# Causal convolution and ELU block: band read without a reversing copy, w_in in three pieces, live rows only, halo zeroed earlier

## The chip, the cores and the metric

The kernel runs on one core of one Trainium2 chip. The metric is the device time of the slowest core, which here is the only one, in microseconds (us). Runs of one kernel agree within about 0.3%. A profiled execution has its own span, which is 2.1 to 2.4 us shorter than the time of the same run, so spans are compared with spans and times with times.

The engines by their names in the profile: PE multiplies matrices, and PEld is its loading of weights; ACT, DVE and POOL compute element by element; SP only issues transfers. A transfer (DMA) is carried by up to 16 DMA engines and counts up a semaphore, on which an instruction that needs the data waits. "Head" below is the time before group 1 starts, and "halo" the 6 rows of zeros ahead of a sequence.

## The reference

x is [8, 4096, 192] in float32. Each of 8 heads of 24 channels is filtered along the sequence with 7 taps (a softmax of its row of `weight`), causally, with zeros ahead of each of the 8 sequences. The result, 32768 rows of 192, goes through two matmuls with an ELU between them:

```python
x_pad = np.concatenate([np.zeros((B, pad, D)), x], axis=1)      # pad = 6
idx = np.arange(S)[:, None] + np.arange(K)[None, :]
x_unf = x_pad[:, idx, :].reshape(B, S, K, H, group)
out = np.einsum('hk,bskhg->bshg', softmax(weight), x_unf)       # then [32768, 192]
h = out @ w_in                                                  # 192 -> 2048
g = np.where(h > 0.0, h, np.exp(np.minimum(h, 0.0)) - 1.0)
return g @ w_out                                                # 2048 -> 192
```

## The kernel before

The 32768 rows are worked through in 32 groups of 1024 rows. A group has 16 steps; step n = 16 s + i makes 128 of the 2048 hidden columns for group s. In each step PE makes h (`H<-att,w_in`), ACT the exponential, POOL the clamp, DVE joins them into gT, and some steps later PE multiplies gT by w_out. The convolution is a matmul too: rows of x (`xg`, windows of 118 rows that overlap by 6, 112 new ones each) against a band matrix `Tm` that holds each head's taps shifted by one from partition to partition. It is made one to two groups ahead; group 0 is done differently, and the first convolution by `Tm` stands in step 7.

The band is built in DRAM. The tap row goes there between zeros, and one transfer reads it with a step of one element per partition. That gives it reversed, so DVE turns it round:

```python
sy.dma_start(bass.AP(tensor=taps.tensor, offset=CW, ap=[[CW, HEADS], [1, CW]]), zt[:, :]).then_inc(s_band, 16)
W(s_band, 32)
sy.dma_start(Tr[:, :, :].rearrange("p h e -> p (h e)"),
    bass.AP(tensor=taps.tensor, offset=TAP + 1, ap=[[1, P], [1, HEADS * CW]])).then_inc(s_band, 16)
...
W(s_band, 48)                                       # DVE, before its first gT
v.tensor_copy(Tm[:], Tr[:, :, ::-1]).then_inc(s_tm)
```

POOL's queue loads and casts the weights and the first two groups of x, in this order, before POOL's first clamp:

```python
W(s_wd, 16)
load_w_in(0, (0, 1))            # columns 0:512, both partition halves
load_w_in(1, (0, 1))            # columns 512:2048
load_x(1, 0); load_x(1, 1)      # 128 rows x 5 windows each
g.dma_start(w_out ...)
load_x(2, 0); load_x(2, 1)
for n in range(NP):
    if i == X_PAD and s + 2 < NS and (s + 2) % SPB == 0:   # X_PAD = 8
        pad_x(s + 2)            # zero the 6 halo rows of a sequence's first group
    ...                         # two clamps
```

From the fourth group on, POOL casts x into DRAM (`x_cast`), and SP loads it from there, 128 rows of four windows and 70 of the fifth:

```python
for w0, w1, rows in ((0, WPG - 1, P), (WPG - 1, WPG, GS - TOK * (WPG - 1) + PAD)):
    sy.dma_start(xg[0:rows, s % NXB, v0 + w0 : v0 + w1, :],
        bass.AP(tensor=xb.tensor, offset=(row + TOK * w0) * D,
                ap=[[D, rows], [TOK * D, w1 - w0], [1, D]])).then_inc(s_xq[s % NXB][part], 16)
```

Of the kernel before, what the change touches and what calls it, by code (L numbers as in the profile page):

```python
# [12 lines left out]
P = 128  # L13
HP = 64
# [11 lines left out]
GS = 512  # L26
SUP = 2 * GS
PAD = KSIZE - 1
NXB = 2
NE = 4  # L30
NG3 = 2
# [3 lines left out]
    ((0, (0, 15, 8, 9)), (1, (6, 6, 7, 13))),  # L35
)
RUN = 4
WCOLS = ((0, 512), (512, 2048))
Q_PART = (0,) * 4 + (1,) * 12
WARM = (9, 1)  # L40

CONV_AT = ((0, 1, 1, 0), (4, 1, 1, 1), (9, 2, 0, 0), (12, 2, 0, 1))
# [4 lines left out]
QUAD = 4  # L47
XTW = 136
HALO = 2
X_PAD, X_COPY, X_LOAD = 8, 3, 15  # L50
X_LATE = (13, 18)


def bass_lightweight_conv__then__act_elu_kernel(
# [160 lines left out]
            t, half = divmod(n_half - 1, 2)  # L215
            previous[n_half // 2, n_half % 2, 0, g] = (t, half, 0, g)

    taps = nc.dram_tensor("conv_taps", ((HEADS + 2) * CW,), BF16).ap()

    xb = nc.dram_tensor("x_cast", (NT, D), BF16).ap()  # L220

    with ExitStack() as stack:
        def sbuf(name, shape, dt):
            return stack.enter_context(nc.sbuf_tensor(name, shape, dt))
# [4 lines left out]
        def sema(name):  # L229
            return stack.enter_context(nc.semaphore(name))  # L230
# [11 lines left out]
        whr = sbuf("whr", [HEADS, 1], FP32)  # L242
        sel = sbuf("sel", [HEADS, P], BF16)
        xg = sbuf("xg", [P, NXB, 2 * WPG, D], BF16)
        Tr = sbuf("Tr", [P, HEADS, CW], BF16)
        Tm = sbuf("Tm", [P, HEADS, CW], BF16)
        csb = sbuf("csb", [P, 2, 3 * 2 * WPG * HP], BF16)
        att = sbuf("att", [P, 2, 3, WPG * TOK], BF16)
# [9 lines left out]
        H = psum("H", [P, 3, 2 * GS])  # L258
        ops = psum("ops", [P, 2, GS])

        s_w = [sema(f"s_w{i}") for i in range(3)]
        s_wd = sema("s_wd")
        s_xl = [sema(f"s_xl{i}") for i in range(2)]
        s_xh = sema("s_xh")
        s_xha = sema("s_xha")
        s_wp = sema("s_wp")
        s_wb = sema("s_wb")
        s_tm = sema("s_tm")
        s_xb = [sema(f"s_xb{i}") for i in range(2)]
        s_xq = [[sema(f"s_xq{i}_{g}") for g in range(2)] for i in range(NXB)]  # L270
        s_id = sema("s_id")
# [42 lines left out]

        def x_ready(W, s, part):
            if s <= NXB:
                W(s_x[s % NXB][part], 16)
            else:
                W(s_xq[s % NXB][part], 32 * ((s - 1) // NXB))

# [73 lines left out]
        @block.gpsimd  # L394
        def _gpsimd(g: bass.BassGpSimd):
            W = Waits(g)

            def load_x(s, part):
                g.dma_start(  # L399
                    xg[:, s % NXB, WPG * part : WPG * (part + 1), :],  # L400
                    bass.AP(
                        tensor=x_flat.tensor,
                        offset=(s * SUP + GS * part - PAD) * D,
                        ap=[[D, P], [TOK * D, WPG], [1, D]],
                    ),
                ).then_inc(s_x[s % NXB][part], 16)

            def pad_x(s):
                x_ready(W, s, 0)
                g.memset(xg[0:PAD, s % NXB, 0, :], 0.0).then_inc(s_z)  # L410

            def copy_x(s):
                W(s_cv, 4 * (s - NXB - 1) + 1)
                if s == NXB + 1:
                    g.dma_start(  # L415
                        xb[s * SUP - 8 : s * SUP, :], x_flat[s * SUP - 8 : s * SUP, :]
                    ).then_inc(s_xb[s % 2], 16)
                g.dma_start(  # L418
                    xb[s * SUP : (s + 1) * SUP, :].rearrange("(p t) d -> p (t d)", p=P),
                    x_flat[s * SUP : (s + 1) * SUP, :].rearrange("(p t) d -> p (t d)", p=P),  # L420
                ).then_inc(s_xb[s % 2], 16)

            def load_w_in(k, halves):
                c0, c1 = WCOLS[k]
                for r in halves:
                    g.dma_start(  # L426
                        w_in[HP * r : HP * (r + 1), :, c0:c1],
                        moe_w_in.rearrange("(p j) f -> p j f", j=3)[:, :, c0:c1],
                    ).then_inc(s_w[k], 16)

            W(s_one, 1)
            g.affine_select(
                out=ident[:],
                in_=ident[:],
                pattern=[[-1, P]],
                compare_op=ALU.is_equal,
                fill=0.0,
                base=0,
                channel_multiplier=1,
            ).then_inc(s_id)  # L440
            g.affine_select(
                out=sel[:].rearrange("p (r h c) -> p r h c", r=2, h=HEADS),
                in_=sel[:].rearrange("p (r h c) -> p r h c", r=2, h=HEADS),
                pattern=[[0, 2], [-1, HEADS], [0, 8]],
                compare_op=ALU.is_equal,
                fill=0.0,
                base=0,
                channel_multiplier=1,
            ).then_inc(s_id)
            W(s_wd, 16)  # L450
            load_w_in(0, (0, 1))
            load_w_in(1, (0, 1))
            load_x(1, 0)
            load_x(1, 1)
            g.dma_start(
                w_out.rearrange("p (q r) d -> p q (r d)", r=RUN),
                moe_w_out.rearrange("(q p r) d -> p q (r d)", p=FC, r=RUN),
            ).then_inc(s_w[2], 16)
            load_x(2, 0)
            load_x(2, 1)  # L460
            for n in range(NP):
                s, i = divmod(n, NQ)
                if i == X_PAD and s + 2 < NS and (s + 2) % SPB == 0:
                    pad_x(s + 2)
                if i == X_COPY and s and s + 3 < NS:
                    copy_x(s + 3)
                if n == X_LATE[0]:
                    copy_x(3)
                for u in range(2):
                    W(s_exp, 2 * n + u + 1)  # L470
                    g.tensor_scalar(  # L471
                        out=E[:, n % NE, u, :],
                        in0=E[:, n % NE, u, :],
                        scalar1=1.0,
                        scalar2=0.0,
                        op0=ALU.min,
                        op1=ALU.max,
                    ).then_inc(s_clp)
# [72 lines left out]
        def _vector(v):  # L551
# [17 lines left out]
            W(s_v, 4)  # L569
            v.tensor_scalar(  # L570
                out=zt[:, TAP : TAP + KSIZE],
                in0=whe[:],
                scalar1=whr[:, 0:1],
                scalar2=None,
                op0=ALU.mult,
            ).then_inc(s_wp)
            W(s_xl[1], 16)
            v.tensor_copy(xh[:, 1, :, :], xf[:, 1, :, :]).then_inc(s_xh)
            W(s_wb, 1)
            v.tensor_tensor(  # L580
                Dg[:, 1:8, :],
                mask[:, :].unsqueeze(1).to_broadcast([P, KSIZE, HP]),
                H[:, 2, 0:KSIZE].unsqueeze(2).to_broadcast([P, KSIZE, HP]),
                ALU.mult,
            ).then_inc(s_D)
            W(s_tp, 3)
# [7 lines left out]
            v.tensor_copy(  # L594
                att[:, 0, 2, GS // 2 : GS], H[:, 1, GS : GS + GS // 2]
            ).then_inc(s_hd)
            W(s_band, 48)
            v.tensor_copy(Tm[:], Tr[:, :, ::-1]).then_inc(s_tm)  # L598
            for x_, op in enumerate(steps):
                if x_ in stops:  # L600
                    acc = acc_of(op)
# [20 lines left out]
        def _tensor(pe):  # L622
# [75 lines left out]
            for x_, op in enumerate(steps):  # L698
# [10 lines left out]
                elif op[0] == "c":  # L709
# [3 lines left out]
                    if hh == 0 and second:  # L713
                        W(s_cs, 2 * m + b + 1)
                    elif hh == 0:
                        if m == 0:
                            W(s_tm, 1)
                            if b:
                                W(s_cv, 1)
                        for part in range(2):  # L720
                            x_ready(W, s, part)
                        W(s_z, z_need[s])
                        if m >= OPS_CONV:
                            wait_bank()
                        elif m:
                            W(s_ce, 2 * (m - 1) + b + 1)
# [14 lines left out]
                elif op[0] == "h":  # L741
# [3 lines left out]
                        W(s_ha, (1, 1, 2)[j])  # L745
                        W(s_hd, (0, 1, 2)[j])
                    if j == 0:
                        W(s_w[Q_PART[q]], 32)
                        W(s_att[s % 2], 16 * ((s + 1) // 2))
                        wait_bank()  # L750
                    ins = pe.matmul(  # L751
# [13 lines left out]
                else:  # L765
                    _, item, rt, g = op
                    t, half, q, kb, turned = item
                    acc = acc_of(op)
                    W(s_w[2], 16)
                    W(s_tt, 2 * (NQ * t + q) + g + 1)  # L770
                    at_end = acc[:2] == (last, 1)
                    if x_ in begins:
# [24 lines left out]
        def _sync(sy):  # L797
# [2 lines left out]
            load_first(sy, 1)  # L800
            W(s_zw, 1)
            sy.dma_start(
                bass.AP(tensor=taps.tensor, offset=0, ap=[[(HEADS + 1) * CW, 2], [1, CW]]),
                zw[0:2, 0:CW],
            ).then_inc(s_band, 16)
            W(s_wp, 1)
            sy.dma_start(
                bass.AP(tensor=taps.tensor, offset=CW, ap=[[CW, HEADS], [1, CW]]), zt[:, :]
            ).then_inc(s_band, 16)
            W(s_band, 32)  # L810
            sy.dma_start(
                Tr[:, :, :].rearrange("p h e -> p (h e)"),
                bass.AP(tensor=taps.tensor, offset=TAP + 1, ap=[[1, P], [1, HEADS * CW]]),
            ).then_inc(s_band, 16)

            def load_cast(s):
                W(s_cv, 4 * (s - NXB))
# [2 lines left out]
                    W(s_xb[(s - 1) % 2], 16 * ((s - 2) // 2 + ((s - 1) % 2)))  # L820
                for part in range(2):
                    row = s * SUP + GS * part - PAD
                    for w0, w1, rows in ((0, WPG - 1, P), (WPG - 1, WPG, GS - TOK * (WPG - 1) + PAD)):
                        v0 = WPG * part
                        sy.dma_start(
                            xg[0:rows, s % NXB, v0 + w0 : v0 + w1, :],
                            bass.AP(
                                tensor=xb.tensor,
                                offset=(row + TOK * w0) * D,
                                ap=[[D, rows], [TOK * D, w1 - w0], [1, D]],  # L830
                            ),
                        ).then_inc(s_xq[s % NXB][part], 16)
# [56 lines left out]
```

## Time and profile before

| before | |
|---|---|
| time | 733.9 us, median of 4 runs (733.21 to 734.47) |
| span of the profiled run | 733.0 us |
| first convolution by `Tm` starts | 23.7 us |
| step 16 (group 1) starts | 37.6 us |
| a group of 16 steps | 21.91 us; 22.64 where a sequence begins |

The starts of steps and groups are read from the first-matmul instructions in the trace. The page's busy time of each engine and its PE row by fortieths of the span come first.

```profile
PE 717.8 (98%) x11866; PEld 640.9 (87%) x11866; DVE 652.7 (89%) x1044; ACT 657.2 (90%) x1286; POOL 630.5 (86%) x1076
...
PE   6999999999999999999999999999999999999997
```

PE is busy all along except in the first slice. There is little to win outside the head and the few places where PE stands still. Those places show when the span is cut into groups. This is the view by stretches of the kernel before: the stretch, its length, the busy us of PE, PEld, DVE, ACT and POOL with their instructions, the granted clock, the DMA share and GB/s.

```profile
37.60:59.40 21.80, 21.80 (x373) 20.64 (x370) 19.37 (x32) 20.69 (x40) 19.27 (x33) 1.00 0.55 108
59.40:82.00 22.60, 22.05 (x372) 19.68 (x369) 20.33 (x33) 20.49 (x40) 19.60 (x35) 1.00 0.46 103
82.00:103.90 21.90, 21.90 (x373) 19.77 (x370) 20.18 (x33) 20.38 (x40) 19.43 (x34) 1.00 0.43 96
```

The middle group, in which the halo of group 4 is zeroed, is 0.7 us longer, and PE is idle for most of that. In the other two PE has no gap at all.

### The profile page before, as it was taken

How to read it: one execution, taken by the hardware profiler on the slowest of the kernel's cores; microseconds unless marked ns; L12 is line 12 of the kernel's file. 1: busy time of each engine (PE TensorE's matmuls, PEld its weight loads, DVE VectorE, ACT ScalarE, POOL GpSimd, SP SyncE). 2: the span in 40 equal slices, each digit the busy share in tenths (PEclk: the TensorE clock that was granted, in tenths of full speed). 3: DMA queues.
4: the chain of work that ended last, by engine and by line, in shares of the span. 5: the costliest groups of instructions: out<-in, count | busy, mean ns of one | idle time of the engine just before them, and what ended most of it. 6: DMA issues, size and time to landing. Idle time of an engine off the chain costs nothing.

```text
span 733.0 us, 28722 instructions
## 1 busy us (share of the span) xinstructions
PE 717.8 (98%) x11866; PEld 640.9 (87%) x11866; DVE 652.7 (89%) x1044; ACT 657.2 (90%) x1286; POOL 630.5 (86%) x1076
## 2 busy tenths in 40 slices
PE   6999999999999999999999999999999999999997
PEld 3598999888999898998998989998898989898997
DVE  3899899999999899998999999999899999999994
ACT  4898999989999999999999989999999989999993
POOL 6889888888888898888898888898888888888893
PEclk9899999999999999999999999999999999999999
DMA  9755334445445544335554445464345453532212
GB/s 177 110 93 114 70 93 115 103 81 98 86 94 114 91 92 106 78 94 114 89 95 99 86 94 114 84 100 97 81 99 115 80 104 86 100 93 70 57 36 66
DMA packets 128959, 69.12 MB, mean 94 GB/s; under 512 B 93932, under 2 KB 127596, under 8 KB 128364
## 3 DMA queue, kind: packets, MB, share of 16 engines
q1 hardware_dynamic: 123596, 52.04, 30.3%
q0 software_dynamic: 4944, 14.75, 14.4%
q8 instruction: 93, 1.52, 0.9%
q10 hardware_dynamic: 288, 0.49, 0.2%
q14 instruction: 38, 0.31, 0.1%
HBM read 43.51 MB, written 36.57 MB: 109 GB/s over the span
## 4 chain that ended last, share of the span: by engine, by line
PE 94%; DMA 2%; ACT 2%; POOL 1%; issue 1%; DVE 0%; ACTq 0%
PE ops L785 50%; PE H L751 40%; PE H L729 3%; DMA Tr<-conv_taps 1%; ACT E L543 1%; POOL E L471 1%; PE H L785 1%; DMA conv_taps<-zt 0%; DVE gT L612 0%; POOL xg L410 0%; ACT L484 0%; ACT csb L521 0%; PE ops L701 0%; POOL x_cast L415 0%; POOL x_cast L418 0%
## 5 line engine op out<-in xcount | busy, mean ns | idle before, releaser
L612 DVE SCALAR_TENSOR_TENSOR gT<-E,H 128x512 f16<-128x512 f32 x1024 | 646.5, 683 | 59.9 <-POOL E L471 51.2
L471 POOL TENSOR_SCALAR E<-E 128x512 f32<-128x512 f32 x1024 | 607.0, 616 | 90.2 <-ACT E L543 86.4
L543 ACT ACTIVATE E<-H 128x512 f32<-128x512 f32 x1024 | 566.8, 613 | 58.3 <-PE H L751 53.8
L751 PE MATMUL H<-att,w_in 64*128 64x512 bf16 x3072 | 612.2, 379 | 5.1 <-DVE gT L612 4.3
L785 PE MATMUL ops<-w_out,gT 64*128 64x192 f16 x8064 | 594.6, 243 | 0.0
L785 PEld LDWEIGHTS ops<-w_out,gT 64*128 64x128 f16 x8064 | 523.7, 94 | 41.6 <-PE ops L785 26.2
L751 PEld LDWEIGHTS H<-att,w_in 64*128 64x128 bf16 x3072 | 293.1, 111 | 20.3 <-DVE gT L612 7.6
L729 PE MATMUL H<-xg,Tm 64*128 64x240 bf16 x480 | 87.6, 262 | 4.1 <-POOL xg L410 3.8
L521 ACT ACTIVATE csb<-H 128x480 bf16<-128x480 f32 x120 | 70.5, 588 | 0.0
L513 ACT ACTIVATE osb<-ops 128x384 f32<-128x384 f32 x125 | 61.1, 488 | 7.3 <-PE ops L785 5.7
L729 PEld LDWEIGHTS H<-xg,Tm 64*128 64x128 bf16 x480 | 39.7, 94 | 19.0 <-issue 6.6
L418 POOL DMA_DIRECT2D x_cast<-in_x_dram x29 | 15.7, 540 | 0.0
L785 PE MATMUL H<-w_out,gT 64*128 64x192 f16 x128 | 6.5, 243 | 0.0
L785 PEld LDWEIGHTS H<-w_out,gT 64*128 64x128 f16 x128 | 5.8, 94 | 0.0
L701 PE MATMUL ops<-zw 64*128 64x512 bf16 x12 | 5.7, 502 | 0.0
L598 DVE COPY Tm<-Tr 128x1024 bf16<-128x1024 bf16 x1 | 0.4, 427 | 5.7 <-DMA Tr<-conv_taps 5.7
L640 PE MATMUL ops<-zw 128*128 128x512 bf16 x9 | 4.0, 631 | 1.3 <-DVE zw L553 1.3
L604 DVE COPY osb<-ops 128x384 f32<-128x384 f32 x1 | 0.6, 558 | 4.3 <-PE ops L785 4.3
L640 PEld LDWEIGHTS ops<-zw 128*128 128x128 bf16 x9 | 1.2, 142 | 3.2 <-issue 1.9
L399 POOL DMA_DIRECT2D xg<-in_x_dram x4 | 3.5, 877 | 0.0
L729 PE MATMUL ops<-xg,Tm 64*128 64x240 bf16 x16 | 3.0, 265 | 0.4 <-ACT csb L521 0.3
L426 POOL DMA_DIRECT2D w_in<-in_moe_w_in_dram x4 | 2.7, 682 | 0.3 <-DMA wh<-in_weight_dram 0.3
(50 smaller groups left out, 30.6 us busy)
## 6 DMA issues: line engine op xcount, KB each, us to landing
out_dram<-osb SPq DMA_DIRECT2D x126, 192.0 KB, 3.2
x_cast<-in_x_dram POOLq DMA_DIRECT2D x29, 384.0 KB, 5.1
xg<-x_cast SPq DMA_DIRECT2D x58, 192.0 KB
xg<-x_cast SPq DMA_DIRECT2D x58, 26.2 KB
w_in<-in_moe_w_in_dram POOLq DMA_DIRECT2D x2, 576.0 KB, 11.7
xg<-in_x_dram POOLq DMA_DIRECT2D x4, 240.0 KB, 15.3
w_out<-in_moe_w_out_dram POOLq DMA_DIRECT2D x1, 768.0 KB, 16.4
att<-csb SPq DMA_TRANSPOSE x31, 5.9
```

The costliest lines, as they stand in the source:

```text
L399: g.dma_start(xg[:, s % NXB, WPG * part : WPG * (part + 1), :], bass.AP(tensor=x_flat.tensor, offset=(s * SUP + GS * part - PAD) * D, ap=[ ...
L418: g.dma_start(xb[s * SUP : (s + 1) * SUP, :].rearrange("(p t) d -> p (t d)", p=P), x_flat[s * SUP : (s + 1) * SUP, :].rearrange("(p t) d - ...
L471: g.tensor_scalar(out=E[:, n % NE, u, :], in0=E[:, n % NE, u, :], scalar1=1.0, scalar2=0.0, op0=ALU.min, op1=ALU.max,).then_inc(s_clp)
L513: a.activation(*out_pieces(acc), ACT.Copy).then_inc(s_oev)
L521: return a.activation(csb[:, s % 2, :].rearrange("p (j v h i) -> p h j v i", j=3, v=2 * WPG, h=HEADS)[:, h0 : h0 + HB], bank_of(("c", m, b ...
L543: a.activation(E[:, n % NE, u, :], bank_of(op[:3]), ACT.Exp).then_inc(s_exp)
L612: v.scalar_tensor_tensor(out=gT[:, s % NG3, q, u, :], in0=E[:, n % NE, u, :], scalar=1.0, in1=bank_of(op[:3]), op0=ALU.subtract, op1=ALU.m ...
L640: pe.matmul(ops[:, 0, :], zw[:, 0:P], zw[:], start=True, stop=True)
L701: pe.matmul(ops[:, 1 - rt, :], zw[HP * rt : HP * (rt + 1), 0:P], zw[HP * rt : HP * (rt + 1), :], start=True, stop=True, tile_position=(HP ...
L729: ins = pe.matmul(bank_of(op[:3])[:, n1 * hh : n1 * (hh + 1)], Tm[HP * rt : HP * (rt + 1), h, :], xg[HP * rt : HP * (rt + 1), s % NXB, :, ...
L751: ins = pe.matmul(bank_of(op[:3]), w_in[HP * r : HP * (r + 1), j, RUN * FC * (q // RUN) + q % RUN : RUN * FC * (q // RUN + 1) : RUN,], att ...
L785: ins = pe.matmul(to[:, d0 : d0 + D], gT[HP * rt : HP * (rt + 1), t % NG3, q, g, t0 : t0 + P], w_out[HP * rt : HP * (rt + 1), q, :], start ...
```

## The change

It means to start the main loop sooner and to take a wait out of every fourth group. The core of the diff, with cuts marked:

```diff
+PARTS = ((0, 4, TOK + PAD), (4, WPG, GS - 4 * TOK + PAD))        # 118 and 70 rows
-WCOLS = ((0, 512), (512, 2048))
+WCOLS = ((0, 512), (512, 1024), (1024, 2048))
-X_PAD, X_COPY, X_LOAD = 8, 3, 15
+X_PAD, X_COPY, X_LOAD = 5, 3, 15
-    taps = nc.dram_tensor("conv_taps", ((HEADS + 2) * CW,), BF16).ap()
+    taps = nc.dram_tensor("conv_taps", (2 * (HEADS + 2) * CW,), BF16).ap()
 ...
+                row, v0 = s * SUP + GS * part - PAD, WPG * part
+                for w0, w1, rows in PARTS:                        # POOL, early loads of x
+                    g.dma_start(xg[0:rows, s % NXB, v0 + w0 : v0 + w1, :], ...)
 ...
+            g.memset(xg[HP:P, 0, :, :]..., 0.0).then_inc(s_xz)    # and one on DVE
 ...
             load_w_in(0, (0, 1))
+            load_w_in(2, (0,))
             load_w_in(1, (0, 1))
 ...
-            W(s_band, 48)
-            v.tensor_copy(Tm[:], Tr[:, :, ::-1]).then_inc(s_tm)
 ...
             sy.dma_start(
-                Tr[:, :, :].rearrange("p h e -> p (h e)"),
-                bass.AP(tensor=taps.tensor, offset=TAP + 1, ap=[[1, P], [1, HEADS * CW]]),
+                Tm[:, :, :].rearrange("p h e -> p (h e)"),
+                bass.AP(tensor=taps.tensor, offset=CW + TAP + KSIZE - 1, ap=[[(HEADS + 2) * CW - HP, 2], [-1, HP], [1, HEADS * CW]]),
             ).then_inc(s_band, 16)
+            c0, c1 = WCOLS[2]
+            W(s_w[2], 16)
+            sy.dma_start(w_in[HP:P, :, c0:c1], w_in[0:HP, :, c0:c1]).then_inc(s_wc, 16)
 ...
-                    for w0, w1, rows in ((0, WPG - 1, P), (WPG - 1, WPG, GS - TOK * (WPG - 1) + PAD)):
+                    for w0, w1, rows in PARTS:                    # SP, steady loads of x
```

The order of the compute instructions on PE, ACT and DVE stays as it was, except for the copy that goes and the memset that comes on DVE.

More of the change, by code (lines that the diff above doesn't have):

```diff
@@ L37 @@
 RUN = 4
-WCOLS = ((0, 512), (512, 2048))
-Q_PART = (0,) * 4 + (1,) * 12
+WCOLS = ((0, 512), (512, 1024), (1024, 2048))
+Q_PART = (0,) * 4 + (1,) * 4 + (2,) * 8
 WARM = (9, 1)
@@ L244, in bass_lightweight_conv__then__act_elu_kernel @@
         xg = sbuf("xg", [P, NXB, 2 * WPG, D], BF16)
-        Tr = sbuf("Tr", [P, HEADS, CW], BF16)
         Tm = sbuf("Tm", [P, HEADS, CW], BF16)
@@ L259, in bass_lightweight_conv__then__act_elu_kernel @@
         ops = psum("ops", [P, 2, GS])
-        s_w = [sema(f"s_w{i}") for i in range(3)]
+        s_w = [sema(f"s_w{i}") for i in range(4)]
+        s_wc = sema("s_wc")
+        s_xz = sema("s_xz")
         s_wd = sema("s_wd")
@@ L267, in bass_lightweight_conv__then__act_elu_kernel @@
         s_wb = sema("s_wb")
-        s_tm = sema("s_tm")
         s_xb = [sema(f"s_xb{i}") for i in range(2)]
@@ L316, in x_ready @@
             if s <= NXB:
-                W(s_x[s % NXB][part], 16)
+                W(s_x[s % NXB][part], 32)
             else:
@@ L398, in load_x @@
             def load_x(s, part):
-                g.dma_start(
-                    xg[:, s % NXB, WPG * part : WPG * (part + 1), :],
-                    bass.AP(
-                        tensor=x_flat.tensor,
-                        offset=(s * SUP + GS * part - PAD) * D,
-                        ap=[[D, P], [TOK * D, WPG], [1, D]],
-                    ),
-                ).then_inc(s_x[s % NXB][part], 16)
+                row, v0 = s * SUP + GS * part - PAD, WPG * part
+                for w0, w1, rows in PARTS:
+                    g.dma_start(
+                        xg[0:rows, s % NXB, v0 + w0 : v0 + w1, :],
+                        bass.AP(
+                            tensor=x_flat.tensor,
+                            offset=(row + TOK * w0) * D,
+                            ap=[[D, rows], [TOK * D, w1 - w0], [1, D]],
+                        ),
+                    ).then_inc(s_x[s % NXB][part], 16)
             def pad_x(s):
@@ L429, in load_w_in @@
                     ).then_inc(s_w[k], 16)
+            g.memset(xg[HP:P, 0, :, :].rearrange("p w d -> p (w d)").bitcast(FP32), 0.0).then_inc(s_xz)
+            W(s_xz, 1)
             W(s_one, 1)
@@ L451, in _gpsimd @@
             load_w_in(0, (0, 1))
+            load_w_in(2, (0,))
             load_w_in(1, (0, 1))
+            W(s_xz, 2)
             load_x(1, 0)
@@ L457, in _gpsimd @@
                 moe_w_out.rearrange("(q p r) d -> p q (r d)", p=FC, r=RUN),
-            ).then_inc(s_w[2], 16)
+            ).then_inc(s_w[3], 16)
             load_x(2, 0)
@@ L571, in _vector @@
                 out=zt[:, TAP : TAP + KSIZE],
-                in0=whe[:],
+                in0=whe[:, ::-1],
                 scalar1=whr[:, 0:1],
@@ L576, in _vector @@
             ).then_inc(s_wp)
+            v.memset(xg[HP:P, 1, :, :].rearrange("p w d -> p (w d)").bitcast(FP32), 0.0).then_inc(s_xz)
             W(s_xl[1], 16)
@@ L582, in _vector @@
                 mask[:, :].unsqueeze(1).to_broadcast([P, KSIZE, HP]),
-                H[:, 2, 0:KSIZE].unsqueeze(2).to_broadcast([P, KSIZE, HP]),
+                H[:, 2, KSIZE - 1 :: -1].unsqueeze(2).to_broadcast([P, KSIZE, HP]),
                 ALU.mult,
@@ L716, in _tensor @@
                         if m == 0:
-                            W(s_tm, 1)
+                            W(s_band, 48)
                             if b:
@@ L747, in _tensor @@
                     if j == 0:
-                        W(s_w[Q_PART[q]], 32)
+                        if Q_PART[q] < 2:
+                            W(s_w[Q_PART[q]], 32)
+                        else:
+                            W(s_wc if r else s_w[2], 16)
                         W(s_att[s % 2], 16 * ((s + 1) // 2))
@@ L768, in _tensor @@
                     acc = acc_of(op)
-                    W(s_w[2], 16)
+                    W(s_w[3], 16)
                     W(s_tt, 2 * (NQ * t + q) + g + 1)
@@ L802, in _sync @@
             sy.dma_start(
-                bass.AP(tensor=taps.tensor, offset=0, ap=[[(HEADS + 1) * CW, 2], [1, CW]]),
-                zw[0:2, 0:CW],
+                bass.AP(tensor=taps.tensor, offset=0, ap=[[(HEADS + 2) * CW, 2], [(HEADS + 1) * CW, 2], [1, CW]]),
+                zw[0:2, 0 : 2 * CW].rearrange("p (a e) -> p a e", a=2),
             ).then_inc(s_band, 16)
@@ L807, in _sync @@
             sy.dma_start(
-                bass.AP(tensor=taps.tensor, offset=CW, ap=[[CW, HEADS], [1, CW]]), zt[:, :]
+                bass.AP(tensor=taps.tensor, offset=CW, ap=[[CW, HEADS], [(HEADS + 2) * CW, 2], [1, CW]]),
+                zt[:, :].unsqueeze(1).to_broadcast([HEADS, 2, CW]),
             ).then_inc(s_band, 16)
@@ L822, in load_cast @@
                     row = s * SUP + GS * part - PAD
-                    for w0, w1, rows in ((0, WPG - 1, P), (WPG - 1, WPG, GS - TOK * (WPG - 1) + PAD)):
-                        v0 = WPG * part
+                    v0 = WPG * part
+                    for w0, w1, rows in PARTS:
                         sy.dma_start(
```

## The prediction

> **What bounds the kernel now.** I read the chain of work that ended last first, by line: 50% of the span is the output matmul (L785), 40% the first matmul (L751), 3% the convolution matmul (L729). The table of engines has PE busy 98%. So the middle is bound by PE, and a change pays only where PE stands idle: in the head, and at waits that PE[...] cannot pass. The first fence is the chain by engine, the second is from the list of waits (who waited for whom: us in total, times, longest).
>
> ```profile
> PE 94%; DMA 2%; ACT 2%; POOL 1%; issue 1%; DVE 0%; ACTq 0%
> ```
>
> ```profile
> DVE Tm L598 <- DMA Tr<-conv_taps: 5.7, 1, 5.7
> PE H L751 <- DVE gT L612: 4.3, 3, 3.7
> PE H L729 <- POOL xg L410: 3.8, 7, 0.6
> ```
>
> Two waits touch the change: one in the head (DVE waits 5.7 us for the band, and PE then 3.7 us for DVE), and seven near 0.55 us each, where PE waits for the halo of zeros. The chain in order of time, 10 to 28 us, shows how the first works:
>
> ```profile
> 7.27 9.02 DMA Tr<-conv_taps
> 16.31 0.43 DVE Tm L598
> 16.74 0.61 DVE gT L612
> 17.39 1.64 PE H L751 x5
> ```
>
> DVE sits on the reversing copy until 16.3 us although POOL's first clamp ended at 13.1; three pairs of banks are full, so PE is idle from 13.7 to 17.39. The third view was the tile view of w_in, and beside it the page's list of DMA issues (times, size, and where known us to landing):
>
> ```profile
> L426 POOL DMA_DIRECT2D w_in<-in_moe_w_in_dram x4: 627/633/836, 2.5 to 4.6; - x4
> ...
> DMA to landing us min/median/max: 4.9/8.9/13.1
> ```
>
> ```profile
> xg<-x_cast SPq DMA_DIRECT2D x58, 192.0 KB
> xg<-x_cast SPq DMA_DIRECT2D x58, 26.2 KB
> ```
>
> The last w_in transfer, issued at 4.6, lands at 4.6 + 13.1 = 17.7: the fifth step (n=4) could not have begun before that anyway. Removing the DVE wait alone would gain almost nothing; that is why the diff also cuts w_in in three.
>
> **What the Trainium skill says.** "DMA: Bandwidth & Descriptors", section "Why a DMA increments its semaphore by 16 and not by 1": a DMA issued from SP runs on k engines, the largest k up to 16 that divides the slowest dimension of both sides; 128 rows give 16, 100 give 10, 127 give 1. The trace agrees as far as it can: each pair of cast loads (128 and 70 rows) leaves 31 semaphore updates, 16 + 14 + 1, and the three transfers of the tap row and the band leave 28, (2+1) + (8+1) + 16. It is also why the two lines above have no landing time. But 70 rows would give 14 under a rule of equal shares of five rows too, so 118 rows are not decided by this trace: 2 by the divisor rule, 15 by shares. For SWDGE (POOL) the same section has a measured exception that shares by sixteenths; no line here tests it.
>
> Same page, section "Queues, rings and completion order": each engine takes turns between the rings that have work, and each ring is in order. The trace agrees: the band's 128 packets of 2 KB have a mean of 104 ns in the packet records, so eight per engine are 0.8 us of work, yet issued at 7.27 they began at 10.8 and the semaphore was full at 16.3, between the weight packets of POOL's queue.
>
> "TensorE: Matmul & The Clock Gate", section "What's actually happening": after about 3.4 us idle the clock halves. The trace agrees: after PE's 3.7 us the granted clock is 0.50 from 17.4 to 22.0.
>
> **The change part by part.**
>
> Reversing copy: removes 0.43 us of DVE and its wait. The tap product is written reversed by a negative step, same size. The first gT could start at 13.1 instead of 16.65.
>
> w_in: first two column pieces whole, of the third only half is loaded; SP copies it to the other partitions. POOL's queue carries 0.39 MB less before step n=4. The old transfers three and four, 0.59 MB each, took from 10.8 to 17.7, 0.17 MB a us; less 0.39 MB is 2.3 us, so n=4 may start near 15.5. With three steps of about 1.35 us, PE asks for the convolution (n=7) near 19.5, against 23.74 before. Worth up to 4.2 us if nothing else is late.
>
> Band: the compiled source pattern is [2][64][1024], its slowest dimension 2. By the page's rule k is 2: 64 packets on each of two engines instead of 8 on each of 16. From 10.5 on they take turns with POOL's queue: 26 turns beside weight packets (about 250 ns a pair, 6.5 us), the other 38 beside x and w_out packets (150 to 280 ns a pair, 6 to 10 us). Landing: 10.5 + 6.5 + 6 to 10 = 23 to 27 us. The convolution wants it at 19.5. The w_in copy stands behind it in the same ring, so n=8 can be held about 1 us more. Head: the 4.2 us are eaten, and 0 to 3 us may be lost on top; if the early x loads are narrow as well (118 rows), up to 5. I take +2.
>
> Zero memsets: POOL and DVE get one each of 64x960 f32, about 1 us. POOL was idle 1.03 us before its first select and DVE 1.51 us before the second cast, so both hide. POOL issues 5 + 8 + 1 DMAs instead of 4 + 4 + 1, about 0.7 us each, so it ends near 12.3 instead of 9.4; its first clamp was at 12.5. Hidden, barely.
>
> Halo three steps sooner: by the stretches between load issues, a group with a pad takes 22.6 us and one without 21.9 to 22.0. Seven of them: 7 x 0.6 = -4.3 us. It holds if the first half of x has landed by then, about 12.2 us after its load's issue.
>
> Live rows in the steady loads: 118 x 4 rows of 384 B. If k is 2, engines 0 and 1 have 236 packets each per half, plus 5 each for the 70-row loads: 482 against 74. In the stretch 38.7 to 42 us, 1131 packets took 52.7% of 16 x 3.3 us, 24.6 ns each. 482 x 24.6 = 11.9 us, plus 1.1 to the first packet and 0.5 to the semaphore: 13.5 us after issue. The cast copy of x (24 KB packets, 2.6 us, one per engine) falls in 9.1 us after the load issue: up to 16.1. Before, issue at 122.26 and the convolution that reads it at 138.21: 15.95 us are there. So the steady state is on a knife's edge; I take it as just hidden, with +3 us for groups that miss. The first such load is tighter: issue 38.69, need 49.83, 11.1 us. It misses by 2.4 to 5: +4.
>
> Sum: 733.5 + 2 (head) + 4 (first cast load) + 3 (steady) - 4.3 (halo) = 738.
>
> **The rivals.**
>
> Wide transfers: the pieces run on 15 or 16 engines despite their shapes. Then the head gains 4.2, the halo 4.3, and the loads move 8% fewer rows: 725. For it: the change is evidently meant so, and the 70-row load tells nothing against it. Against it: the page names the narrow cases and the tap-row transfer of 2 rows leaves only 2 + 1 updates.
>
> Narrow and not hidden: a packet costs more than 24.6 ns when an engine gets 236 in a row, because bursts of 32 are all this trace has. Each ns more adds 0.48 us per load, and over 28 groups 13.5 us. With 28 ns and the cast copy in series, PE waits about 1.8 us in every group: 738 + 50 = 788. For it: engines 0 and 1 would carry some 20 us of packets in each 22 us group. Against it: median packets are 22 ns, and with two engines nothing else crowds the memory.
>
> Only the head counts: DVE's wait was followed by an equal wait for w_in, and the band is late in either case, so all that stays is the halo: 729.
>
> **Range and chances.** Wide at 15%, narrow and just hidden (728 to 746) at 52%, narrow with a wait in each group at 33%, with a long tail. Range 726 to 780. Two per cent is 14.7 us: faster would need more than both gains together, 0.02. Slower needs 0.5 us per group, which is most of the third case: 0.28. The rest, 0.70, is same.
>
> **What would show it.** Right: the semaphore of the steady loads gets (2+1) + (14+1) updates per pair; PE's wait before L729 is on the band near 23 to 27 us and once on xg near 50; the pad waits are gone; DVE's first gT starts near 13.1. In the page's waits a line of the conv matmul waiting for xg with some 28 entries means the second rival; no DMA wait before L729 at all, and n=7 near 19.5, the first. I would be plainly wrong if the halo wait came back, if POOL's longer issue held its first clamp, or if the transposes queued behind the loads on engines 0 and 1 came late for the next group.

## The result

| | before | after |
|---|---|---|
| time, median of 4 runs | 733.9 us | 740.16 us (739.98 to 740.58) |
| span of the profiled run | 733.0 us | 738.2 us |
| POOL's first clamp starts | 12.5 us | 18.5 us |
| first convolution by `Tm` | 23.7 us | 30.8 us |
| step 16 starts | 37.6 us | 45.7 us |
| group 1 takes | 21.74 us | 23.84 us |
| groups in which a halo is zeroed | 22.64 us | 21.91 us |

The ratio is 1.0087, 95% interval 1.0069 to 1.0104. Ratios here are the mean time of one kernel's fast runs over that of the other's of the same rounds, so they are not quite the ratio of the medians quoted. It is slower by 0.9%, inside the 2% that count as the same, and well outside the noise.

The two spans differ by 5.2 us. Step 16 starts 8.1 us later, group 1 costs 2.1 us more, and seven groups are 0.73 us shorter each, -5.1: together +5.1. All other groups are equal to 0.02 us. So there are three things to explain, and two of the three lie before 70 us. The times differ by 6.3 us, not by 5.2: the profiled run of the kernel before took 735.3 us, 1.4 above the median of its timed runs, so about 1 us of the loss is not in this account.

The waits of PE in the changed kernel, from its list of waits (us in total, times, longest), with the lines that answer to those of before:

```profile
PE H L760 <- DVE gT L618: 6.9, 4, 6.2
...
PE ops L735 <- DMA xg<-in_x_dram: 5.2, 1, 5.2
...
PE H L735 <- issue: 1.8, 1, 1.8
```

DVE no longer waits for the band and the convolution no longer waits for the halo. In their place PE's wait for DVE has grown from 3.7 to 6.2 us, and the first convolution waits 5.2 us for x. "Issue" in the last line means that the profile shows no releaser. The transfer behind it has no landing time, for the reason given in the prediction, but the trace's semaphore records have its last update at 59.94 and the convolution starts at 60.03. It is the first load of cast x.

Why DVE came so late is seen on POOL. This is its timeline in the changed kernel (start, length, instruction):

```profile
5.92 5.95 POOL L402 DMA_DIRECT2D xg<-in_x_dram  x4
11.86 0.81 POOL L462 DMA_DIRECT2D w_out<-in_moe_w_out_dram  x1
12.62 5.94 POOL L402 DMA_DIRECT2D xg<-in_x_dram  x4
18.53 4.85 POOL L478 TENSOR_SCALAR E<-E 128x512 f32<-128x512 f32 x8
```

POOL is still issuing loads of x at 18.5 us. Before, it was done at 9.4 and its first clamp ran at 12.5. The tile view of xg has the durations (min/median/max of one issue, first and last start); first the kernel before, then the changed one:

```profile
L399 POOL DMA_DIRECT2D xg<-in_x_dram x4: 855/868/917, 5.2 to 8.6; - x4
```

```profile
L402 POOL DMA_DIRECT2D xg<-in_x_dram x8: 542/1511/2463, 5.9 to 18.0; - x8
```

A transfer of 118 rows by 4 windows takes POOL 2.46 us to issue, though it has fewer rows than the 128 by 5 windows that took 0.87. The median mixes it with the small transfers of 70 rows, 0.54 to 0.60 us each. The chain in order of time then shows what set the first convolution:

```profile
11.33 19.32 DMA xg<-in_x_dram
30.79 0.35 PE ops L735
```

The last load of group 1's x, 70 rows issued at 11.33, landed at 30.65, and the convolution of step 7 started at once. The band had been there since 21.3. After the wait the granted clock was 0.50 from 30.8 to 36 us, and from the first convolution to step 16 PE took 14.9 us where it had taken 13.9, so a slower clock may be about 1 of the 8.1 us.

The groups after that, in the view by stretches of the changed kernel, answer to the three groups shown of before:

```profile
45.70:69.60 23.90, 22.06 (x373) 20.34 (x370) 19.47 (x32) 20.76 (x40) 19.25 (x33) 1.00 0.38 90
69.60:91.50 21.90, 21.90 (x373) 19.73 (x370) 20.20 (x33) 20.38 (x40) 19.55 (x35) 1.00 0.41 95
91.50:113.40 21.90, 21.90 (x373) 19.78 (x371) 20.20 (x33) 20.38 (x40) 19.39 (x34) 1.00 0.43 95
```

The halo group has lost its gap, and group 1 has got one of 1.8 us.

### The profile page after: what moved, and what is told of

Its sections match the earlier page's. It is cut to its first block, busy times and chain, and to the rows that moved or that the text cites. A ratio compares the mean times of both kernels' runs of the same rounds, so it can differ in the third digit from the quotient of the medians.

```text
span 738.2 us, 28732 instructions
## 1 busy us (share of the span) xinstructions
PE 717.1 (97%) x11866; PEld 641.0 (87%) x11866; DVE 652.3 (88%) x1044; ACT 656.3 (89%) x1286; POOL 638.8 (87%) x1082
## 4 chain that ended last, share of the span: by engine, by line
PE 94%; DMA 3%; POOL 2%; issue 1%; ACT 0%; DVE 0%; ACTq 0%; POOLq 0%
PE ops L794 50%; PE H L760 40%; PE H L735 3%; DMA xg<-in_x_dram 3%; POOL xg L402 1%; PE H L794 1%; POOL w_in L429 0%; POOL E L478 0%; PE ops L735 0%; ACT E L550 0%; POOL xg L434 0%; ACT csb L528 0%; DVE gT L618 0%; POOL x_cast L418 0%; POOL x_cast L421 0%
## 5 line engine op out<-in xcount | busy, mean ns | idle before, releaser
L421 POOL DMA_DIRECT2D x_cast<-in_x_dram x29 | 15.2, 524 | 0.0
L402 POOL DMA_DIRECT2D xg<-in_x_dram x8 | 11.9, 1513 | 0.0
L735 PE MATMUL ops<-xg,Tm 64*128 64x240 bf16 x16 | 4.5, 380 | 5.3 <-DMA xg<-in_x_dram 5.2
L735 PEld LDWEIGHTS ops<-xg,Tm 64*128 64x128 bf16 x16 | 1.7, 118 | 7.1 <-issue 5.6
```

The source lines that it names most:

```text
L402: g.dma_start(xg[0:rows, s % NXB, v0 + w0 : v0 + w1, :], bass.AP(tensor=x_flat.tensor, offset=(row + TOK * w0) * D, ap=[[D, rows], [TOK * ...
L421: g.dma_start(xb[s * SUP : (s + 1) * SUP, :].rearrange("(p t) d -> p (t d)", p=P), x_flat[s * SUP : (s + 1) * SUP, :].rearrange("(p t) d - ...
L735: ins = pe.matmul(bank_of(op[:3])[:, n1 * hh : n1 * (hh + 1)], Tm[HP * rt : HP * (rt + 1), h, :], xg[HP * rt : HP * (rt + 1), s % NXB, :, ...
```

## The experiments

The theory after the result was: the narrow shapes cost the head, above all those of POOL; the band on two engines is late but nobody waits for it; the narrow steady loads are hidden but for the first; the halo is worth 5 us. Ten kernels were run, all correct. "Wide" below means that the transfer can use all 16 engines. The first four ran on one chip beside a before of 734.06 us. The changed kernel was not run again beside them: differences from it are between medians of different sessions, and worked out from the ratios they come out up to 0.8 us different.

### a1: early loads of x wide

```diff
-                for w0, w1, rows in PARTS:
+                for w0, w1, rows in ((0, 4, P), PARTS[1]):        # POOL
```

> Changed kernel, only the early loads of x on POOL back at 128 rows (four windows in one transfer, the fifth with 70 rows in a second one as in the change). My theory: the shape costs, since 118 rows go to two engines and POOL wrote four such transfers in about 2.4 us each. Then POOL's first clamp starts near 12.5 instead of 18.5, x lands before 20, the band (21.3) becomes the last wait before the first convolution, which starts near 21.5 instead of 30.8; time 731 to 732. Rival one: the number of transfers (8 instead of 4) and POOL's queue order cost, not their shape: first clamp still after 16, time 738 to 740. Rival two: the band on two engines holds the head: no gain, 740.

Measured: 733.42 us, 6.7 less than the changed kernel; ratio to before 0.9991 (0.9976 to 1.0005). The first clamp starts at 12.48, so rival one is out: there are still eight transfers, only their shape is different. The time is above the 731 to 732 that I expected. The tile view:

```profile
L402 POOL DMA_DIRECT2D xg<-in_x_dram x8: 556/698/815, 5.7 to 11.1; - x8
```

But the convolution started at 24.5, not at 21.5, and it was not the band that it waited for, which was there at 21.85. The timeline of PE, with the idle time before and what ended it:

```profile
24.48 0.35 PE L735 MATMUL ops<-xg,Tm 64*128 64x240 bf16 x1 [5.42 <-DMA xg<-in_x_dram]
```

The semaphore records tell where x was. Of the 32 updates of the second half of x, 28 came by 17.02 and the last four at 24.16 to 24.34. Each transfer gives one update per engine, and there were two transfers, so two engines were 7 us behind the rest. The band goes to two engines as well. The trace does not number the engines, so that they are the same two is inferred. In a4 below, with the band on 16 engines, no two lag: the last updates of the second half of x come at 17.74, 17.95 and 19.19.

### a2: steady loads wide

```diff
-                    for w0, w1, rows in PARTS:
+                    for w0, w1, rows in ((0, 4, P), PARTS[1]):    # SP
```

> Changed kernel, only the steady loads of the cast x on SP back at 128 rows. My theory: in the steady state the narrow loads are fully hidden (last packet about 11 us after issue, need at 16), only the first one is late by about 2 us: 738, the wait before the convolution at 60 us gone, all later groups as long as before. Rival: narrow loads on engines 0 and 1 cost something in every group: 735 or less.

Measured: 738.49 us, 1.7 less than the changed kernel. Group 1 is 21.75 us instead of 23.84, and all later groups are 21.91 in both. As expected: the narrow loads cost one wait of 2.1 us and nothing in the steady state.

### a3: band wide

The obvious source pattern, one step of -1 over 128 partitions, does not compile. Sixteen copies of the tap row in DRAM allow a positive outer step of 16:

```diff
-    taps = nc.dram_tensor("conv_taps", (2 * (HEADS + 2) * CW,), BF16).ap()
+    taps = nc.dram_tensor("conv_taps", (16 * (HEADS + 2) * CW,), BF16).ap()
 ...                                          # both writes of the row: 16 copies instead of 2
-    ap=[[(HEADS + 2) * CW - HP, 2], [-1, HP], [1, HEADS * CW]]
+    ap=[[(HEADS + 2) * CW - 8, 16], [-1, 8], [1, HEADS * CW]]
```

> Changed kernel, only the band on 16 engines: sixteen copies of the tap row in DRAM and a source pattern of [16][8][1024] instead of [2][64][1024]. My theory: the band lands near 16 instead of 21.3, but x lands at 30.7, so nothing changes: 739.5 to 740.5. Rival: the band is what holds the head, gain of 3 to 6 us: 734 to 737.

Measured: 734.89 us, 5.3 less than the changed kernel. My theory was wrong here. The band lands at 15.4, and with that x lands at 25.69 instead of 30.65; the convolution starts at 25.9 instead of 30.8. Nobody waited for the band itself, but its narrow shape made x late. How it did so is argued and not traced: its 64 packets on each of two engines would take turns with the packets of x there. At the 104 ns that a packet of the band took in the kernel before, 64 of them are 6.7 us (an estimate), about the lag of the two engines in a1. So in the changed kernel the first convolution was held by x, and x by the band and its own shape together. In the part that is left to x's shape (25.7 here, 19.2 in a4) the later issue and the two engines are mixed, and no run separates them. POOL's clamp is as late here as in the changed kernel (19.1), and it now counts: with step 3 at 20.5, PE reached step 7 only at 25.8, when x was there:

```profile
25.77 0.40 PE L760 MATMUL H<-att,w_in 64*128 64x512 bf16 x1 [0.20 <-DVE gT L618]
25.87 0.36 PE L735 MATMUL ops<-xg,Tm 64*128 64x240 bf16 x2
```

### a4: all three wide

a2 and a3 together, and the early x as single transfers of 128 rows by 5 windows as before:

```diff
-                for w0, w1, rows in PARTS:
+                for w0, w1, rows in ((0, WPG, P),):               # POOL, one semaphore count less
```

> Changed kernel with all three wide: early x as single transfers of 128 rows by 5 windows, cast x at 128 rows, band on 16 engines; everything else of the change stays. My theory: the three costs go, what is left is the gain of the earlier halo (about 5 us) and of a head that starts the fourth step near 14 instead of 17.4: 725 to 729. Rival: removing the reversing copy gives nothing, since something else arrives as late: 729 to 731.

Measured: 725.81 us (725.36 to 726.41), ratio to before 0.9888 (0.9873 to 0.9902). This beats both kernels: 8.2 us under before and 14.4 under the changed kernel. The three parts alone gave 6.7, 1.7 and 5.3, sum 13.7, so they nearly add up. (a4 also joins the two early loads of a half into one, which no run tests alone.) Step 3 starts at 13.8, the first convolution at 19.3, step 16 at 33.0 (before: 37.6). PE's clock is full throughout the head. The page's row of engines:

```profile
PE 714.4 (99%) x11866; PEld 638.5 (88%) x11866; DVE 652.0 (90%) x1044; ACT 656.0 (91%) x1286; POOL 631.9 (87%) x1078
```

### b1: only the halo sooner, in the kernel before

```diff
-X_PAD, X_COPY, X_LOAD = 8, 3, 15
+X_PAD, X_COPY, X_LOAD = 5, 3, 15
```

> Kernel before with only the halo zeroed at step 5 instead of 8. My theory: seven waits of the convolution for the halo go, each worth 0.6 to 0.7 us of a group: 728.5 to 730, no wait on the halo in the list. Rival: POOL's memset merely moves and holds a clamp elsewhere: 733 to 734.5.

Measured: 728.45 us beside 734.04, ratio 0.9924 (0.9909 to 0.9939). All groups are 21.91 us and no wait for the halo is left. One number in the diff gives 5.6 us, of which the seven groups explain 5.1. That is the larger part of what a4 gains (8.2). The spans of the two profiled runs differ by 6.9, and the other 1.9 were chance in the head, where the edit changes nothing: the band happened to land 0.8 us sooner, PE was idle 3.2 us rather than 3.7, and the clock did not fall. The view by stretches, first b1, then before:

```profile
17.00:21.50 4.50, 4.30 (x29) 1.45 (x29) 4.50 (x8) 3.26 (x6) 2.86 (x5) 1.00 1.27 206
```

```profile
17.40:22.00 4.60, 4.60 (x22) 2.94 (x24) 4.19 (x8) 2.40 (x4) 1.94 (x4) 0.50 1.27 206
```

Clock 1.00 against 0.50 in the same stretch of the same work. This agrees with the Trainium skill, "TensorE: Matmul & The Clock Gate", section "What's actually happening", which has the clock halve after an idle window of about 3.4 us: 3.2 us of idle PE left it at 1.00 here, and 3.7 us took it to 0.50.

### b2: only the reversing copy gone, in the kernel before

The sixteen copies of a3, the taps written reversed, DVE's copy and its wait taken out; w_in, x and halo as before.

> Kernel before with only the reversing copy gone: the reversed band is read straight into Tm on 16 engines (sixteen copies of the tap row); w_in still in two column pieces, x and halo as before. My theory, as predicted: the second piece of w_in lands at 17.6 whatever DVE does, so the fourth step starts near 14 but the fifth near 17.7 instead of 19.1, and the gain is about 1.4 us: 732 to 733. Rival: DVE's wait was the whole of it, gain 3.5 us or more: under 731.

Measured: 733.18 us beside 734.04 with five rounds, ratio 0.9984 (0.9971 to 0.9997). That is 0.9 us by the medians, 1.2 by the ratio: just above the range that I gave, and far from the rival's 3.5 and more. Its runs spread over 732.03 to 734.46, more than usual, and the profiled one is the quickest, so its span of 729.7, 3.3 under that of before, flatters it. Step 3 starts at 13.7 now, and the timeline of PE has the next wait:

```profile
17.36 0.40 PE L747 MATMUL H<-att,w_in 64*128 64x512 bf16 x1 [2.18 <-DMA w_in<-in_moe_w_in_dram]
```

The wait for DVE is gone and a wait for w_in stands in its place, as the prediction said.

### a6: early loads at 124 rows, four engines

```diff
-                for w0, w1, rows in PARTS:
+                for w0, w1, rows in ((0, 4, 124), PARTS[1]):      # POOL
```

> Changed kernel with POOL's early loads at 124 rows: the largest divisor up to 16 is then 4. My theory: POOL writes as many entries for each idle engine as a working one gets (472 descriptors of 118 rows came with 14 x 236 packets of 4 bytes), so here 12 x 124 = 1488 small packets per transfer, about 5950 in all plus some 264, and one such issue takes about 1.5 us, between 0.80 (128 rows) and 2.46 (118): first clamp near 15.5, time 734 to 738. Rival: only the divisor rule for 118 is odd and 124 rows are spread like 128: small packets near 260, issue 0.8 us, first clamp 12.5, time 733.4 as with 128 rows.

Measured: 736.27 us, first clamp at 15.27, an issue of 124 rows 1.56 to 1.61 us. The view of DMA queues from 0 to 42 us gives the packets, megabytes and share of POOL's queue. In order: before, changed kernel, a6, a1.

```profile
q0 software_dynamic: 4048, 3.74, 59.3%
```

```profile
q0 software_dynamic: 17120, 2.85, 80.4%
```

```profile
q0 software_dynamic: 10015, 3.26, 66.4%
```

```profile
q0 software_dynamic: 4128, 3.26, 54.6%
```

The changed kernel has about 13,000 packets more in POOL's queue than the wide a1 while its early x moves fewer bytes. In the packet records 13,480 of its packets have 4 bytes. 224 of them are the semaphore updates of these 14 transfers. The other 13,256 are 4 x 14 x 236 for the transfers of 118 rows plus 4 x 2 x 5 for those of 70 rows, exactly, as if every engine that gets no data got as many small packets as a working one gets rows. a6 has 6232 up to 40 us; 16 belong to the first small cast of x, and the other 6216 are again exact, 4 x 12 x 124 + 4 x 2 x 5 + 224. The issue time follows the count. From 512 entries (0.80 us) to 16 x 236 = 3776 (2.46 us) it grows by 0.51 ns an entry, and 1984 entries would then take 1.55. The count is always 16 times the rows of a working engine, so these runs cannot tell the writing of entries from a wait for the fullest engine; that the four issues of 118 rows took 2.42 to 2.46 us, whatever had been queued before them, speaks for the writing.

### a7: steady loads at 127 rows, one engine

```diff
-                    for w0, w1, rows in PARTS:
+                    for w0, w1, rows in ((0, 4, 127), PARTS[1]):  # SP
```

> Changed kernel with the steady loads at 127 rows, which is prime, so one engine. My theory: packets of one engine start 18.9 ns apart, so 2 x 508 of them take 19.2 us, plus 1.6 before the first and 0.5 to the semaphore, and up to 2.6 for the cast copy: 21.3 to 23.9 us after issue against 16 needed. Each of 28 groups then waits 5 to 8 us: 880 to 970 us, with a wait of the convolution for x in every group. Rival: a single ring with a deep queue hides it, or the rate of one engine is higher when it is alone: under 760.

Measured: 1010.76 us in a single run whose state is unknown, 38% above before, and above my range. The mechanism is as expected and the size is not. The list of waits:

```profile
PE H L735 <- issue: 215.5, 29, 11.2
```

215.5 us over 29 is 7.4 us a time, within the 5 to 8 expected, and the last packet started 22.9 us after the issue in most groups. But the span grew by 270 us over that of the changed kernel, 9.3 in each of 29 groups. Part of the rest is the clock, which falls after such an idle time. The stretch after one of these waits:

```profile
100.50:104.00 3.50, 3.45 (x35) 3.06 (x37) 0.69 (x1) 1.77 (x3) 0.61 (x1) 0.56 0.72 109
```

How the remainder divides between the slow clock and the refilling of the loop was not measured. What the run settles is that hiding has an edge, and that two engines are just on the good side of it.

### a8: all wide, w_in loaded whole

```diff
             load_w_in(0, (0, 1))
-            load_w_in(2, (0,))
             load_w_in(1, (0, 1))
+            load_w_in(2, (0, 1))
 ...                                          # the copy on SP and its wait go
```

> The all-wide kernel with w_in loaded whole by POOL in three column pieces in their order of use, without the half load and SP's copy. My theory: the queue carries 0.39 MB more before x, at 0.17 MB a us that is 2.3 us; the second piece is there earlier (step 5 near 14.6), but x for the first convolution lands near 21.5 instead of 19.2, so the first convolution moves by about 2 us: 727 to 729 against 725.8. Rival: the copy is no help, since SP's queue competes for the same engines: 725 to 726.5.

Measured: 728.42 us beside 734.32, 2.6 more than a4 (1.8 by the ratios). Step 4 starts at 14.7, sooner than a4's 15.9, but x lands at 22.0 and the convolution waits for it:

```profile
22.17 0.36 PE L735 MATMUL ops<-xg,Tm 64*128 64x240 bf16 x1 [3.74 <-DMA xg<-in_x_dram]
```

So the half load with a copy on the chip is a good part of the change.

### a5: the changed kernel with the halo late

```diff
-X_PAD, X_COPY, X_LOAD = 5, 3, 15
+X_PAD, X_COPY, X_LOAD = 8, 3, 15
```

> Changed kernel with the halo back at step 8. My theory: seven groups become 22.64 us long again instead of 21.91, so 5.1 us more: 744.5 to 746. Rival: in the changed kernel the halo is no longer in the way, as the head has moved everything: 740 to 741.

Measured: 744.62 us beside 734.32 (743.99 to 745.25), 4.5 more than the changed kernel (3.7 by the ratios), in the range that I gave. The groups with a halo are 22.64 us again. Group 1 is 22.99 here, not 23.84: the first cast load landed at 59.23 instead of 59.94, so it was a little less late in this run.

## Why the prediction was right or wrong

**The total.** 738 was predicted; the span became 738.2 and the time 740.16. That closeness is luck: of the four terms of the sum three had the wrong size, and their errors cancel.

**The bound.** Right. PE outside the head has no gap but those named, and in every kernel but a7 the changes of time lie in the head, in group 1, or in the halo groups.

**The halo, -4.3.** Right in mechanism, and somewhat larger: 0.73 us in each of seven groups, 5.1. a5 (4.5) and b1 (5.6) show it from both sides. Its condition, that the first half of x has landed in time, held.

**w_in.** Right. All of the second piece was there at 15.06 (predicted 15.5), and a1 without the other hindrances started step 4 at 15.2. b2 confirms that without it the reversing copy is worth only about 1 us, and a8 that the half load is worth about 2.

**The band on two engines.** k was 2: the trace has 15 semaphore updates for the three transfers, (2+1) + (8+1) + (2+1). It landed at 21.3; I had said 23 to 27. The step that failed is what followed from it: that "the convolution wants it" and would wait for the band. It waited for x. The band did harm in a way I had not thought of: its narrow shape made x late, and with a wide band the changed kernel gains 5.3 us (a3).

**POOL's issues, "hidden, barely".** This is the step that was plainly wrong. I took 0.7 us for each issue from the issues of the kernel before, which has none of 118 rows. The narrow ones took 2.46, the clamp started at 18.5 instead of 12.3 to 12.5. I had named this as what would make the prediction wrong, but given it no size. Together with the band it made the head cost 8.1 us where I had put +2, "up to 5".

**The live rows in the steady loads.** k was 2 here as well: each pair of transfers leaves 18 updates, (2+1) + (14+1), as the prediction worked out. The term of +3 for groups that miss measured 0. I had taken 24.6 ns a packet from busy bursts on 16 engines. With two engines working, 52 to 54 packets started in each half microsecond in most of the transfer, 18.9 ns apart on each engine if the two share them evenly, and the last one started about 11 us after the issue, with 16 available. The term of +4 for the first load measured 2.1: it was late, for the reason given, by less. (That the loads ran on "engines 0 and 1", as the prediction has it, is not shown: the trace does not number the engines.)

**The memsets.** Right. They took 0.89 us on POOL and 0.86 on DVE, and the tap product on DVE started at 3.36 us in both kernels.

So the head was underrated by 6, the steady loads and the first one overrated by 5, and the halo underrated by 0.8.

**The rivals.** "Wide transfers", 725, is what a4 made true at 725.8 by giving the transfers shapes that divide by 16. The chance of 0.15 that the change as written was already so came to nothing. "Narrow and not hidden" failed for two engines and holds for one (a7). "Only the head counts" had the right observation, one wait behind the other, but not the costs of the new shapes.

## What to carry to other kernels

Before a transfer is made smaller by leaving rows out, look at what its outermost size divides by: 118 rows instead of 128 put the work on two engines, and made POOL's issue nearly three times as long. A late transfer can harm without anyone waiting for it, so ask what else has to pass through the same engines: the narrow band alone made x land 5 us later. And when several waits in a head end almost together, taking one away shows the next, so all of them have to be moved before the gain appears: here 0.9 us for the reversing copy alone, and about 3 with w_in and wide shapes (the 8.2 of a4 less the 5.1 of the halo).

## What the Trainium skill lacked or had wrong

- "DMA: Bandwidth & Descriptors", section "Why a DMA increments its semaphore by 16 and not by 1": the rule of the largest divisor held on SP for 118 rows (2 engines), 70 (14), 127 (1: 17 updates a pair, (1+1) + (14+1)) and for an outer dimension of 2. The page's exception for SWDGE, shares by sixteenths, did not apply to POOL's casting loads: by the counts of small packets (4 x 14 x 236 and 4 x 12 x 124), 118 rows went to 2 engines and 124 to 4.
- The same section says that with SWDGE all 16 engines post. It does not say that a narrow transfer also makes 4-byte packets, as many as if each idle engine got one for every row a working one gets: 13,256 in the changed kernel, which is 4 x 14 x 236 + 4 x 2 x 5.
- The same page, section "Anatomy of one DMA", calls descriptor generation "small, variable" and says that many can be emitted before it shows. Here it showed: 0.80 us for 512 entries, 1.56 to 1.61 for 1984, 2.46 for 3776, and POOL could compute nothing meanwhile.
- No page says how much longer the issue on SP gets when few engines carry the transfer. The four steady loads of a group took it 1.95 us before, 8.8 us after, and 20.6 with one engine (a7). The SP timelines, first before, then after:

```profile
122.26 1.95 SPq L825 DMA_DIRECT2D xg<-x_cast  x4
```

```profile
131.73 8.81 SPq L839 DMA_DIRECT2D xg<-x_cast  x4
```
